# Causal masks written in bf16 by GpSimd, new issue orders for all engines, and a new placing of unused matmuls in a fused linear-attention and MLP kernel

## The chip, the core and the metric

The kernel runs on one core of a Trainium2 chip. The metric is the device time of one execution in microseconds (us); less is better. The engines are named as in the profile: PE is TensorE (matmuls), with PEld for its weight loads; DVE is VectorE, ACT is ScalarE, POOL is GpSimd, and SP is SyncE, which here only issues DMAs. L430 is line 430 of the kernel before.

## The reference

A linear attention with decay feeds a two-layer MLP. Shapes: q, k, v of 4 batches x 8 heads x 768 positions x 64; lam of 8; w_in 512 x 2048, w_out 2048 x 512, alpha 2048; all f32. The output has 3072 tokens x 512.

```python
def _attn_ref(q, k, v, lam):                 # block = 64
    rel = pos[:, None] - pos[None, :]
    Dmask = np.where(rel >= 0, lam[:, None, None] ** rel[None, :, :], 0.0)
    lam_pow = lam[:, None, None] ** (pos[None, :, None] + 1)
    for b in range(nb):
        intra = np.einsum('bhic,bhjc->bhij', qb, kb) * Dmask[None]
        intra = np.einsum('bhij,bhjd->bhid', intra, vb)
        inter = np.einsum('bhid,bhde->bhie', qb * lam_pow[None], kv_state)
        out[:, :, sl] = intra + inter
        kb_dec = kb * rev_pow[None]
        kv_state = lam_block * kv_state + np.einsum('bhsd,bhse->bhde', kb_dec, vb)

def _moe_ref(x, w_in, w_out, alpha):         # x: 3072 x 512, the heads side by side
    h = x @ w_in
    s = np.sin(alpha * h)
    g = h + s * s / (alpha + 1e-09)
    return g @ w_out
```

## The kernel before, in words

**Attention.** The 3072 tokens are 24 blocks of 128 (six of a batch). q is multiplied by powers of lam at load time and k by inverse powers (`scale_block`, L470, L487, L480, L499), so that inside a block the decay needs only a 0/1 mask; v is only cast to bf16 (L493, L502). Each scaled block is transposed on PE (L541 and L518 for q, L568 for k, with `ident` as the second operand) and copied out by ACT or DVE (L546 to L579). Then come S = the products of k and q (`piece_S`, L620), the mask product on DVE (`Sm`, L631), the state Z = v times k (`piece_Z`, L656 and L664) with its bf16 copy into the block-diagonal tile `Zd` (L674), P = Sm times v (L767), I = q times state (L787), and the copy of the sum to `xT` (L734, L747). The first four blocks, the head, are written out piece by piece; the later ones go through the same steps under other lines (L702, L715, L724).

**Decay factors.** Three iotas on POOL make exponents `E_i` (L413 to L417), a cast makes `E_f` (L419), DVE multiplies by ln(lam) (`lnL`, L443), ACT takes four exponentials (`Lq`, `Lp`, `Lk`, L445 to L451) after a table load and a `warm` activation (L442); another table load for the sine follows them (L452).

**Masks.** There are three masks of 128 x 128: two for the head, where positions are interleaved by four, and one for all later blocks. DVE fills one f32 tile `maskf` with ones (L426), POOL's affine_select zeroes what lies above the diagonal (L430, in halves of 64 rows for the first two masks, so five instructions), and DVE casts each to the bf16 `mask` (L435). The identity is made in the same way (L421, L422, L425). POOL also clears the two `Zd` tiles (L438).

**MLP.** Tokens are cut into six chunks of 512. h is computed by units of four 128 x 128 weight tiles against 512 tokens (`unit_A`, L830) or, where half a chunk is ready, of eight matmuls of 256 tokens (`unit_A2`, L864). For each, ACT takes the sine (`t`, L840 or L874), the square is taken by ACT or POOL (`u`, L844, L845, L878, L879) and DVE adds h and multiplies by 1/alpha (`gT`, L847, L882). The first chunk is multiplied by w_out plainly (`unit_B`, L895 and L909); the others by a scheme with fewer matmuls that works on sums of weights (`weight_sums`, L938) and of tokens (`token_sums`, L961) and products of these (`unit_P`, L983, combined in L1000 to L1029).

**Loads.** All DMAs of inputs go through `load` (L325). SP brings q, k, v of the head, the two f32 halves `ws` of the first quarter of w_in (cast by L394 to the first quarter of `w1`), and then q, k, v of later blocks. The other quarters of `w1` and the four of `w2` are brought by POOL's queue, which casts on the way; an issue of such a load takes its turn in POOL's own order, between its squares.

**What sets the order.** Nothing is issued as it is called. `op(...)` records an operation with what it reads and writes, numbered in the order of the calls; a table `ORDER` for each of PE, ACT, DVE, POOL and SP, written out as numbers, then gives the order in which each engine issues them. An operation that more than one engine can do (casts, copies, squares, scalings) goes to the engine in whose table its number stands. `_settle` merges the tables, and `emit` puts a semaphore wait before each operation that depends on another engine's. A pair `(n, cols)` in PE's table stands for n unused matmuls (`spin`, L1142): 128 x 128 by `cols` columns of the tile `idle`, whose result is overwritten later. `idle` is the first part of `Xs_0`, filled by a memset on DVE (L420).

PE's table before begins with 24 unused matmuls, the transposes of k and q with alpha's in between, then by turns the last transposes of k, S of the four blocks and Z of blocks 0, 1 and 2; then P and I of the head with two unused matmuls of 128 columns ahead of the last I, and then the units of the first chunk.

Of the kernel before, what the change touches and what calls it, by code (L numbers as in the profile page):

```python
# [8 lines left out]
F32 = mybir.dt.float32  # L9
# [26 lines left out]
class _Plan:  # L36

    ORDER = {
# [14 lines left out]
        ),  # L53
        "ACT": (
# [15 lines left out]
        ),  # L70
        "DVE": (
# [15 lines left out]
        ),  # L87
        "POOL": (
# [7 lines left out]
        ),  # L96
# [6 lines left out]
        ),  # L103
    }

# [111 lines left out]
def bass_lightning_attn__then__act_snake_kernel(  # L217
# [40 lines left out]
    with es:  # L258

        def sb(name, shape, dt):  # L260
            return es.enter_context(nc.sbuf_tensor(name, shape, dt))
# [27 lines left out]
        Zc = ring("Zc", 2, [128, 4, D], BF16)  # L289
        Zd = ring("Zd", 2, [128, 4, 128], BF16)  # L290
        mask = ring("mask", 3, [128, 128], BF16)
        maskf = sb("maskf", [128, 3, 128], F32)
        ident = sb("ident", [128, 128], BF16)
        identf = sb("identf", [128, 128], F32)
        lam_bc = sb("lam_bc", [128, H], F32)
# [18 lines left out]
        def _(_unused_eng):  # L314
# [4 lines left out]
            op = P.op  # L319
# [103 lines left out]
                out=identf[:, :], in_=identf[:, :], pattern=[[-1, 128]], compare_op=ALU.not_equal,  # L423
                fill=1.0, base=0, channel_multiplier=1), 0.5, ["identf"], ["identf"])
            op("DVE", lambda e: e.tensor_copy(ident[:, :], identf[:, :]), 0.2, ["identf"], ["ident"])  # L425
            op("DVE", lambda e: e.memset(maskf[:, :, :], 1.0), 0.3, writes=[("maskf", i) for i in range(3)])  # L426
            for i in range(3):
                t, ks = (4, 2) if i < 2 else (2, 1)
                for r in ((0, 64), (64, 128)) if i < 2 else ((0, 128),):
                    part = op("POOL", lambda e, i=i, r=r, t=t, ks=ks: e.affine_select(  # L430
                        out=maskf[r[0]:r[1], i, :], in_=maskf[r[0]:r[1], i, :], pattern=[[1, t], [t, 128 // t]],
                        compare_op=ALU.is_ge, fill=0.0, base=-i if i < 2 else 0, channel_multiplier=-ks), 0.3,
                       [("maskf", i)], [("maskf", i)])
                    part.some = i < 2
                op("DVE", lambda e, i=i: e.tensor_copy(mask[i][:, :], maskf[:, i, :]), 0.2, [("maskf", i)], [("mask", i)])  # L435

            for i in range(2):
                op("POOL", lambda e, i=i: e.memset(Zd[i][:, :, :], 0.0), 0.5, writes=[("Zd", i, 0), ("Zd", i, 1)])  # L438
# [818 lines left out]
```

## Time and profile before

| | before |
|---|---|
| median of 3 runs | 212.92 us (212.35 to 214.85) |
| the profiled execution | 213.46 us, of which the span of its records is 211.7 |
| mean granted clock of TensorE | 0.984 |
| DMA | 33.4 MB in 78,999 packets, mean 158 GB/s |
| busiest groups on PE | L830 68.2 us, L983 59.5 us in three groups, L864 23.1 us |
| the chain that ended last | 70% PE, 7% ACT, 7% DVE, 6% DMA, 5% POOL |

A group row of the profile gives line, engine, operation, output and inputs, and count, then busy time and mean ns of one, then the idle time just before and what ended most of it. A row of the timeline gives start and length in us, engine, line, operation and count, and in brackets the wait before it. A row of the chain gives start, length, engine and line. The granted clock is the share of full speed that the chip's throttle gave to TensorE. The rows that matter are shown where they are used.

### The profile page before, as it was taken

How to read it: one execution, taken by the hardware profiler on the slowest of the kernel's cores; microseconds unless marked ns; L12 is line 12 of the kernel's file. 1: busy time of each engine (PE TensorE's matmuls, PEld its weight loads, DVE VectorE, ACT ScalarE, POOL GpSimd, SP SyncE). 2: the span in 40 equal slices, each digit the busy share in tenths (PEclk: the TensorE clock that was granted, in tenths of full speed). 3: DMA queues.
4: the chain of work that ended last, by engine and by line, in shares of the span. 5: the costliest groups of instructions: out<-in, count | busy, mean ns of one | idle time of the engine just before them, and what ended most of it. 6: DMA issues, size and time to landing. Idle time of an engine off the chain costs nothing.

```text
span 211.7 us, 4834 instructions
## 1 busy us (share of the span) xinstructions
PE 202.7 (96%) x1925; PEld 136.4 (64%) x1947; DVE 169.8 (80%) x297; ACT 154.2 (73%) x281; POOL 127.3 (60%) x135
## 2 busy tenths in 40 slices
PE   6979999999999999999999999999999999999994
PEld 2547644555777777667656666765776665677994
DVE  2795496898989999998878987868788666979772
ACT  4685797636999999896988889767975688866000
POOL 6034266713599999698778999398754449022400
PEclk9995899999999999999999999999999999999999
DMA  5999999998899989997999954306400012100424
GB/s 133 305 313 220 186 231 226 231 205 208 177 230 249 291 181 220 224 201 164 200 289 142 242 125 103 97 3 142 156 3 0 3 50 95 54 5 0 174 83 144
DMA packets 78999, 33.36 MB, mean 158 GB/s; under 512 B 55408, under 2 KB 76160, under 8 KB 78976
## 3 DMA queue, kind: packets, MB, share of 16 engines
q1 hardware_dynamic: 74320, 28.19, 57.5%
q0 software_dynamic: 3696, 3.67, 10.7%
q10 hardware_dynamic: 960, 1.19, 2.1%
q8 instruction: 15, 0.25, 0.5%
q14 instruction: 8, 0.07, 0.1%
HBM read 27.28 MB, written 6.29 MB: 159 GB/s over the span
## 4 chain that ended last, share of the span: by engine, by line
PE 70%; ACT 7%; DVE 7%; DMA 6%; POOL 5%; SPq 2%; issue 2%
PE bank L983 24%; PE bank L830 20%; PE bank L864 8%; PE bank L895 6%; POOL gT L961 4%; DMA v<-in_v_dram 3%; ACT t L840 3%; PE bank L724 2%; DMA out_dram<-osb 2%; PE bank L620 2%; SPq L325 2%; DVE gT L882 2%; DVE gT L847 2%; ACT u L844 2%; PE bank L656 1%
## 5 line engine op out<-in xcount | busy, mean ns | idle before, releaser
L830 PE MATMUL bank<-xT,w 128*128 128x512 bf16 x279 | 68.2, 379 | 1.7 <-issue 0.6
L847 DVE SCALAR_TENSOR_TENSOR gT<-u,rinv,bank 128x512 bf16<-128x512 bf16 x74 | 53.9, 743 | 18.1 <-ACT u L844 14.5
L840 ACT ACTIVATE t<-bank,alpha 128x512 bf16<-128x512 f32 x74 | 49.6, 682 | 18.1 <-PE bank L830 16.0
L830 PEld LDWEIGHTS bank<-xT,w 128*128 128x128 bf16 x296 | 27.5, 98 | 28.0 <-DVE gT L847 1.5
L961 POOL TENSOR_TENSOR gT<-gT 128x512 bf16<-128x512 bf16 x31 | 35.7, 1171 | 11.1 <-DVE Xs L961 10.3
L844 ACT ACTIVATE u<-t 128x512 bf16<-128x512 bf16 x61 | 37.9, 629 | 2.1 <-DVE gT L847 0.5
L631 DVE TENSOR_TENSOR Sm<-bank,mask 128x1024 bf16<-128x1024 f32 x24 | 29.0, 1217 | 0.6 <-PE bank L620 0.5
L961 POOL TENSOR_TENSOR Xs<-gT 128x512 bf16<-128x512 bf16 x20 | 23.1, 1168 | 9.2 <-DVE gT L847 9.2
L845 POOL TENSOR_TENSOR u<-t 128x512 bf16<-128x512 bf16 x13 | 13.6, 1047 | 21.1 <-ACT t L840 21.0
L864 PE MATMUL bank<-xT,w 128*128 128x256 bf16 x176 | 23.1, 280 | 0.1
L882 DVE SCALAR_TENSOR_TENSOR gT<-u,rinv,bank 128x256 bf16<-128x256 bf16 x44 | 18.9, 473 | 3.3 <-ACT u L878 2.2
L983 PE MATMUL bank<-w,gT 128*128 128x256 bf16 (+1 forms) x168 | 20.1, 268 | 0.0
L983 PE MATMUL bank<-ws,gT 128*128 128x256 bf16 x160 | 19.9, 273 | 0.0
L874 ACT ACTIVATE t<-bank,alpha 128x256 bf16<-128x256 f32 x44 | 18.3, 476 | 2.1 <-PE bank L864 1.8
L983 PE MATMUL bank<-w,Xs 128*128 128x256 bf16 (+1 forms) x168 | 19.5, 268 | 0.2 <-DVE osb L1029 0.2
L864 PEld LDWEIGHTS bank<-xT,w 128*128 128x128 bf16 x176 | 16.7, 101 | 3.5 <-ACT xT L734 0.3
L983 PEld LDWEIGHTS bank<-w,Xs 128*128 128x128 bf16 x168 | 15.7, 98 | 3.9 <-DVE osb L1029 0.7
L983 PEld LDWEIGHTS bank<-w,gT 128*128 128x128 bf16 x168 | 15.7, 98 | 3.7
L983 PEld LDWEIGHTS bank<-ws,gT 128*128 128x128 bf16 x160 | 15.4, 98 | 3.8 <-DVE osb L1029 0.4
L499 POOL TENSOR_TENSOR qk<-k,Lk 128x512 bf16<-128x512 f32 x16 | 17.4, 1102 | 0.0
L480 POOL TENSOR_TENSOR qk<-q,Lq 128x512 bf16<-128x512 f32 x16 | 17.2, 1082 | 0.0
L895 PE MATMUL bank<-w,gT 128*128 128x512 bf16 x59 | 15.0, 379 | 0.4 <-issue 0.2
(105 smaller groups left out, 270.9 us busy)
## 6 DMA issues: line engine op xcount, KB each, us to landing
k<-in_k_dram SPq DMA_DIRECT2D x24, 256.0 KB, 4.8
q<-in_q_dram SPq DMA_DIRECT2D x12, 512.0 KB, 5.9
v<-in_v_dram SPq DMA_DIRECT2D x24, 256.0 KB, 5.5
out_dram<-osb SPq DMA_DIRECT2D x18, 256.0 KB, 2.4
w<-in_moe_w_out_dram POOLq DMA_DIRECT2D x4, 512.0 KB, 9.7
w<-in_moe_w_in_dram POOLq DMA_DIRECT2D x3, 512.0 KB, 7.1
ws<-in_moe_w_in_dram SPq DMA_DIRECT2D x2, 512.0 KB, 7.1
out_dram<-osb ACTq DMA_DIRECT2D x8, 128.0 KB, 3.9
```

Of the source, the lines that this page charges most:

```text
L499: lambda e: e.tensor_tensor(qk2[:, j, H:2 * H, :], block32(k32, jl), lk, ALU.mult), 1.05,
L631: op("DVE", lambda e: e.tensor_tensor(Sm[js][:, :, :], banks[:, 512 * b0:512 * b0 + 1024].rearrange("p (c i) -> p c i", i=128), bass.AP(ma ...
L830: ins = e.matmul(ps[hb][:, c0:c1], w1[:, kc, 128 * m:128 * (m + 1)], xT[x][:, kc, c0:c1], start=(kc == 0 and c0 == lo), stop=(kc == NKC - ...
L840: op("ACT", lambda e: e.activation(t16[ju][:, w], ps[hb][:, w], ACTF.Sin, scale=alpha[:, m:m + 1]), 0.69 if hi - lo == TCH else 0.475, [ba ...
L844: lambda e: (e.activation(u16[ju][:, w], t16[ju][:, w], ACTF.Square) if e is nc.scalar else e.tensor_tensor(u16[ju][:, w], t16[ju][:, w], ...
L847: op("DVE", lambda e: e.scalar_tensor_tensor(out=gT[g][:, m, w], in0=u16[ju][:, w], scalar=rinv[:, m:m + 1], in1=ps[hb][:, w], op0=ALU.mul ...
L864: ins = e.matmul(ps[hb][:, 256 * i:256 * i + 256], w1[:, kc, 128 * (m + i):128 * (m + i + 1)], xT[x][:, kc, lo:lo + 256], start=(kc == 0 a ...
L874: op("ACT", lambda e, i=i: e.activation(t16[ju][:, 256 * i:256 * i + 256], ps[hb][:, 256 * i:256 * i + 256], ACTF.Sin, scale=alpha[:, m + ...
L882: op("DVE", lambda e, i=i: e.scalar_tensor_tensor(out=gT[g][:, m + i, lo:lo + 256], in0=u16[ju][:, 256 * i:256 * i + 256], scalar=rinv[:, ...
L895: ins = e.matmul(ps[ob][:, w], gT[g][:, m, 128 * s4:128 * (s4 + 1)], w2[:, m, w], start=(m == 0), stop=(m == NM - 1),)
L961: e.tensor_tensor(dst, in0, in1, alu), 0, rd, wr))
L983: ins = e.matmul(ps[ob][:, lo + d0:lo + d1], lhs, rhs[:, d0:d1], start=first and p == 0, stop=(p == NM // 2 - 1), skip_group_check=True)
```

## The change

1. `maskf` is gone. DVE fills each bf16 `mask[i]` with ones, and POOL's five selects write it in place; the three casts L435 are dropped. Operation numbers from there on fall by one.
2. All five tables are new. In the head: SP loads q ahead of k; on POOL all five selects and both clears of `Zd` stand ahead of `E_f`; POOL casts three of the head's four v tiles and ACT one (two and two before), and takes one k scaling from DVE, which takes a state copy; ACT does the cast of `w1`'s first quarter after the last state copies; on DVE the memset of `idle` is first. POOL's weight loads stand so, by quarter: w1[1], w1[2], w2[0], three squares, w1[3], w2[1], one square, w2[2], one square, w2[3]. Before, it was w1[1], w1[2], w2[0], one square, w1[3], three squares, w2[1], w2[2], three squares, w2[3]. The body's units, pieces and evictions are reordered throughout.
3. Unused matmuls: 18 of 512 columns at the start, 3 of 512 ahead of the first S, 1 of 512 ahead of the third S; before, 23 + 1 of 512 at the start and 2 of 128 ahead of the last I.

```diff
         "PE": (
-            (23, 512), (1, 512), 61, 39, 62, 53, 55, 57, 59, 69, 65, 70, 67, 75, 73, 82, 78, 87, 80, 85, 90, 91,
-            (2, 128), 93, 124, 130, 140, 136, 147, 151, 155, 144, 163, 167, 159, 230, 175, 228, 171, 183, 229,
...
+            (18, 512), 54, 58, 38, 56, 52, 60, 61, (3, 512), 64, 68, 69, 66, (1, 512), 72, 74, 77, 81, 79, 84,
+            86, 89, 92, 90, 123, 129, 139, 143, 135, 150, 146, 154, 158, 166, 162, 174, 228, 227, 170, 229, 178,
...
-        maskf = sb("maskf", [128, 3, 128], F32)
...
-            op("DVE", lambda e: e.memset(maskf[:, :, :], 1.0), 0.3, writes=[("maskf", i) for i in range(3)])
             for i in range(3):
+                op("DVE", lambda e, i=i: e.memset(mask[i][:, :], 1.0), 0.2, writes=[("mask", i)])
                 t, ks = (4, 2) if i < 2 else (2, 1)
                 for r in ((0, 64), (64, 128)) if i < 2 else ((0, 128),):
                     part = op("POOL", lambda e, i=i, r=r, t=t, ks=ks: e.affine_select(
-                        out=maskf[r[0]:r[1], i, :], in_=maskf[r[0]:r[1], i, :], pattern=[[1, t], [t, 128 // t]],
+                        out=mask[i][r[0]:r[1], :], in_=mask[i][r[0]:r[1], :], pattern=[[1, t], [t, 128 // t]],
                         compare_op=ALU.is_ge, fill=0.0, base=-i if i < 2 else 0, channel_multiplier=-ks), 0.3,
-                       [("maskf", i)], [("maskf", i)])
+                       [("mask", i)], [("mask", i)])
                     part.some = i < 2
-                op("DVE", lambda e, i=i: e.tensor_copy(mask[i][:, :], maskf[:, i, :]), 0.2, [("maskf", i)], [("mask", i)])
```

107 rows, old and new, of the table ORDER are left out of this document.

## The prediction

> **What bounds the kernel now.** I read the page first, for the share of each engine and the granted clock in 40 slices.
>
> ```profile
> PE 202.7 (96%) x1925; PEld 136.4 (64%) x1947; DVE 169.8 (80%) x297; ACT 154.2 (73%) x281; POOL 127.3 (60%) x135
> PEclk9995899999999999999999999999999999999999
> ```
>
> TensorE is busy for 96% of the span of 211.7 us, so the body is bound by the number of its matmuls, which the change leaves alone. In the slice from 15.9 us the granted clock is 0.5. Next, the table of stretches, cut where the clock changes (steps of 3.41 us fit; it is low from 16.04 to 22.87).
>
> ```profile
> 5.80:9.21 3.41, 3.41 (x20) 1.64 (x18) 2.73 (x6) 2.07 (x6) 0.00 (x0) 1.00 0.97 298
> 9.21:12.63 3.42, 2.77 (x46) 1.83 (x44) 3.33 (x8) 2.76 (x6) 0.00 (x0) 1.00 1.20 303
> 12.63:16.04 3.41, 2.53 (x68) 1.86 (x68) 3.41 (x3) 2.77 (x7) 1.85 (x3) 1.00 1.13 326
> 16.04:19.45 3.41, 3.13 (x75) 2.34 (x68) 1.51 (x3) 1.77 (x4) 2.06 (x4) 0.50 1.16 224
> 19.45:22.87 3.42, 3.42 (x47) 2.76 (x40) 2.91 (x7) 1.19 (x3) 0.00 (x0) 0.50 1.24 205
> 22.87:40.00 17.13, 16.84 (x86) 8.00 (x87) 11.61 (x19) 14.87 (x27) 10.24 (x11) 1.00 1.16 212
> 60.00:205.00 145.00, 143.04 (x1380) 100.66 (x1395) 122.17 (x215) 112.98 (x204) 101.01 (x96) 1.00 0.59 132
> ```
>
> The second column is PE's busy time, the last three are granted clock, DMA share and GB/s. PE was busy for 2.77 and 2.53 of two steps of 3.41; after the second the clock was halved for 6.83 us. From 22.87 on PE idles 0.29 of 17.13 us, and 1.96 of the 145 us after 60: no reordering of the body can win much. DMA is full to 40 and beyond. The chain of waits of the head, and the first matmuls of the MLP (L864):
>
> ```profile
> 5.88 7.08 DMA v<-in_v_dram
> 13.66 0.63 PE bank L656 x8
> 16.59 1.03 PE bank L656 x8
> 17.63 1.00 PE bank L767 x32
> 18.63 0.54 PE bank L787 x4
> 21.35 2.57 PE bank L864 x16
> 52.81 1.75 PE bank L864 x16
> 37.00 2.59 PE bank L830 x12
> ```
>
> The second load of v lands at 12.96, the state matmuls (L656) follow, and from 16.59 the chain is TensorE alone, at half clock: an L656 group takes 1.03 instead of 0.63, and 16 L864 matmuls take 2.57 where the warm ones at 52.81 take 1.75 (0.87 for a unit of 8; an L830 unit of 4 takes 2.59 / 3 = 0.86).
>
> **The masks.** What is removed, what stays, and what the POOL queue also has to make:
>
> ```profile
> L430 POOL TENSOR_SCALAR_AFFINE_SELECT maskf<-maskf 64x128 f32<-64x128 f32 (+1 forms) x5 | 1.5, 307 | 0.3
> L435 DVE CAST mask<-maskf 128x128 bf16<-128x128 f32 x3 | 0.8, 258 | 0.0
> 3.41 0.29 POOL L419 CAST E_f<-E_i 128x128 f32<-128x128 int32 x1
> 4.13 0.52 POOL L438 MEMSET Zd<- 128x512 bf16 x1
> 5.47 0.20 ACT L442 ACTIVATE warm<-lnlam 128x1 f32<-128x1 f32 x1
> 45.17 1.23 DVE L631 TENSOR_TENSOR Sm<-bank,mask 128x1024 bf16<-128x1024 f32 x1 [0.23 <-PE bank L620]
> ```
>
> Three casts of 0.26 leave VectorE. The last stands ahead of the product at 45.17, which then still waits 0.23 for PE; the others lie in the head, where VectorE waits for the exponentials (below) and for q. On the path they are worth nothing. One memset becomes three smaller ones, ahead of that same wait. The five selects stay, in bf16, a form that no row shows: I bound one between 0.15 (half the f32 row, if bytes counted) and 0.6 (twice it), and take the f32 row's 0.31, the same instruction on as many elements. What hangs on it is the queue: E_f now stands behind all five selects and both Zd memsets, two selects and a memset more than before, 2 x 0.31 + 0.52 = 1.14: its cast ends at 3.70 + 1.14 = 4.84. lnL follows (put at 0.26, a mask cast's elements), ready at 5.1; the exponentials cannot run before the warm activation is through at 5.67. So 0.57 are to spare and the delay costs nothing. At 0.6 a select, five add 1.45: the exponentials 0.9 late, of which I let 0.4 reach the MLP.
>
> **The unused matmuls.** 24 + 2 become 18 + 3 + 1.
>
> ```profile
> 1.93 7.25 PE L1142 MATMUL bank<-Xs 128*128 128x512 bf16 x24 [1.93 <-DVE Xs L420]
> ```
>
> The 24 end at 9.18, 0.30 each. Eighteen end about 1.8 earlier, at 7.4, less the 0.4 by which the memset of their operand comes earlier: 7.0. PE then waits for the first scaled tile, at most the 2.2 until 9.18. The three and the one stand where PE waits for ScalarE's copies, and cost nothing; the two that go stood on the path, 0.2 warm (0.22 each, an L830 matmul).
>
> **The head's order.** SP loads q before k; both land as early together as before, since DMA is full. The first L656 still waits for the second v, now cast by POOL instead of ScalarE: 13.7 again. The next bound is VectorE's four mask products:
>
> ```profile
> 12.59 3.49 DVE L631 TENSOR_TENSOR Sm<-bank,mask 128x1024 bf16<-128x1024 f32 x3
> 16.35 1.23 DVE L631 TENSOR_TENSOR Sm<-bank,mask 128x1024 bf16<-128x1024 f32 x1 [0.27 <-PE bank L620]
> 14.31 0.76 ACT L674 CAST Zd<-bank 64x256 bf16<-64x256 f32 x2 [0.22 <-PE bank L656]
> 16.56 1.04 ACT L394 CAST w<-ws 128x1024 bf16<-128x1024 f32 x1
> ```
>
> VectorE loses a k scaling of 512 columns (to POOL) and gains a state copy of 256; by the products' 1.16 per 1024 columns that is 0.3 net. So the first product starts near 12.2; four in a row and the copy (0.3 to 0.4) end at 12.2 + 4.64 + 0.35 = 17.2, where the old four ended at 17.58. Then one L767 group (1.00 at half clock, 0.5 warm) and two L787 groups (0.27 each warm) end at 18.2. The w1 cast on ScalarE, now behind two more state copies (0.76), ends at 17.60 + 0.76 = 18.4. The MLP starts at 18.4 instead of 21.35, and its first two units take 1.75 instead of 2.57: done at 20.15, not 23.92. That is **3.77 us**, if the clock stays at 1.00. If it halves from 16.04 to 22.87 again, the start is 18.4 + 0.8 for the groups at half clock, 19.2, the two units take twice 1.75 and end at 22.7: 1.2 us.
>
> **Whether the clock stays.** The step that brought the fall was 2.53 busy and the one before it 2.77. The new order puts three unused matmuls (0.65) into the first, which is then full, and one into the second: 2.75, about what the first had before, plus the products and state groups that now come earlier. I take it that the clock stays, at 2 to 1. PE's longest single wait in there was half a us:
>
> ```profile
> PE bank L656 <- ACT Zd L674: 0.8, 2, 0.5
> ```
>
> [...]
>
> **What is late next: the weights.** The body's first part needs w1 and w2 quarter by quarter, which POOL's queue loads between its squares.
>
> ```profile
> 26.37 0.80 POOL L325 DMA_DIRECT2D w<-in_moe_w_in_dram  x1
> 30.94 1.55 POOL L325 DMA_DIRECT2D w<-in_moe_w_out_dram  x2
> L845 POOL TENSOR_TENSOR u<-t 128x512 bf16<-128x512 bf16 x13 | 13.6, 1047 | 21.1 <-ACT t L840 21.0
> w<-in_moe_w_in_dram POOLq DMA_DIRECT2D x1, 512.0 KB, 7.1
> w<-in_moe_w_out_dram POOLq DMA_DIRECT2D x1, 512.0 KB, 7.3
> w<-in_moe_w_out_dram POOLq DMA_DIRECT2D x1, 512.0 KB, 10.6
> w<-in_moe_w_out_dram POOLq DMA_DIRECT2D x1, 512.0 KB, 8.8
> 39.59 0.86 PE bank L895 x4
> 42.90 0.81 PE bank L895 x3
> 48.24 0.81 PE bank L895 x3
> ```
>
> The four loads, with their KB and us to landing, are in order those issued at 26.37 (w1's last quarter, lands 33.5), 30.94 (w2's second, 38.2), about 31.7 (w2's third, 42.3) and 37.3, after three more squares (w2's last, 46.1). The old order first uses w2's second at 39.59, its third at 42.90 and its last a unit after 48.24, at 49.1: slack 1.4, 0.6 and 3.0. So the new order, 3.77 earlier, runs into the loads. Before w2's second quarter it has one L830 unit less (0.86): PE is there at 20.15 + 39.59 - 23.92 - 0.86 = 34.96 and, with landings as before, waits until 38.2, 0.5 ahead of the old kernel. It also wants w2's last quarter earlier: two units (1.72) and a step of attention (1.1, by an L656 group of 0.63 and two L787 groups of 0.27) come after it now. Landing still at 46.1, it lets PE go on at 46.2 with 2.8 still owed: 49.0, level with the old 49.1. **The gain is then what the loads come earlier, x.**
>
> POOL's queue: w1's last and w2's second quarter now follow three squares, one directly after the other. In the old kernel w1's last was issued 26.37 - 21.35 = 5.0 behind the MLP's start, after one square; 0.8 of this was half clock. With two more squares of 1.05 (the L845 row) the new issues come at 18.4 + 4.2 + 2.1 = 24.7 and 25.5, 1.7 and 5.4 earlier. If the loads still wait for all that SP brings, x is 0; if nothing but their issue counted, the 3.77 arrive whole. I take x from the first of the two, **1.7**: the landings lay 4.7, 4.1 and 3.8 apart, so it is the engines that space them (DMA share 1.16), and a queue that starts 1.7 sooner with the same spacing stays 1.7 ahead. 38.2 becomes 36.5, and 34.96 is still below it: the loads, not the head, decide.
>
> SP's queue moves along: q of the next blocks still waits for w1's third quarter, then k, v, v in the old order. Their scalings on VectorE and POOL stand ahead of evictions, so a late k or v would hold those up; I cost it at zero, as DMA brings the same bytes by the same time, and keep it for the slow end. The body's other reorderings have 0.29 + 1.96 of idle to win, or as much to lose; I take zero.
>
> **Sum.** The profiled execution took 213.46 (211.7 of span and 1.76 around it), 0.54 over the median of 212.92. 213.46 - 1.7 = 211.76, or against the median **211.2**. A measurement of this kernel tells about 2% from no change, 4.3 us; this is 0.8%.
>
> **The rivals.**
> 1. The loads land as before (x = 0) and the head's gain is spent waiting for w2: 213.46 + 0.4 of new small waits, 213.3 beside the median. For it: the full DMA engines; against: the earlier issues. 0.2.
> 2. The loads come as early as their issue and the head's 3.77 arrives whole: 209.2. For it: the first gap, 4.7, was wider than the last, 3.8, so there was room. 0.15.
> 3. The clock falls all the same at 16.04: the head gains 1.2, which the loads allow: 211.7. 0.15.
> 4. The slow side: the clock closes a step earlier. Behind the eighteen PE waits up to 2.2 for scaled tiles; if that makes the step from 5.80 count as low, half clock runs from 9.21 to 22.87. Two L656 groups (0.4 more each) and what lies before the MLP slip about as much again: the MLP starts 1.7 later than the old 21.35, at 23.0, its two units are warm and end at 24.8, 0.9 behind the old kernel, and the late E_f's 0.4 comes on top: 214.2. It decides where the step from 5.80 has PE busy for less than the 2.53 that brought the fall, a hole over 0.9. 0.1.
>
> [...]
>
> That the change does not do what it says is possible only as case 3. My forecast holds the remaining 0.4.
>
> **Numbers.** Range: from a body that wins 0.5 beyond case 2 to case 4 with the selects at 0.6 (0.4 more): 208.7 to 214.7, which takes in x from 0 to 3.77. Faster by over 2% is under 208.7: the far end of case 2, 0.13. Slower by over 2% is over 217.2: only if k or v starve for some 5 us behind the bunched weights, 0.07. Within: 0.80.
>
> **What would show it.** Granted clock 1.00 from 12.6 to 23; L656's first group at 13.7; the first MLP group at 18.4; E_f's cast ending before 5.4 and selects near 0.31; w1's last and w2's second quarter issued near 24.7 and 25.5 and landing near 31.8 and 36.5; PE waiting about 1.5 us at the first use of w2's second quarter and little elsewhere. I would be wrong if PE waits for k or v between 40 and 50, if the clock halves before 12.6, or if PE's idle time after 60 differs by more than 1 us from 1.96.

## The result

| | median, us | runs | ratio to before (95% interval) |
|---|---|---|---|
| before | 213.25 | 20 | |
| changed | 215.45 | 20 | 1.0109 (1.008 to 1.0138) |

The change makes the kernel 1.1% slower, 2.3 us. The forecast was 0.8% faster, with a range that ended at 214.7. The profiled execution took 215.03, of which 213.3 is its span. Ratios, here and below, leave out runs that are more than 1.5% above the fastest of the same kernel, while medians take all runs. The table of stretches of the changed kernel (length, busy time of PE, PEld, DVE, ACT, POOL, then granted clock, DMA share, GB/s):

```profile
9.21:12.63 3.42, 3.30 (x62) 2.28 (x61) 3.27 (x7) 2.05 (x5) 1.98 (x3) 1.00 1.20 290
12.63:16.04 3.41, 3.16 (x86) 2.18 (x87) 3.41 (x5) 2.56 (x7) 2.24 (x4) 1.00 1.12 332
16.04:19.45 3.41, 2.13 (x50) 1.46 (x50) 2.86 (x6) 2.76 (x5) 1.13 (x2) 1.00 1.25 229
19.45:22.87 3.42, 2.88 (x14) 2.06 (x14) 0.32 (x2) 0.84 (x2) 0.26 (x1) 0.51 1.24 204
22.87:40.00 17.13, 17.13 (x87) 7.83 (x86) 9.73 (x16) 13.40 (x23) 12.15 (x12) 1.00 1.17 209
40.00:60.00 20.00, 18.40 (x186) 11.19 (x184) 18.84 (x29) 13.33 (x28) 8.24 (x7) 1.00 1.10 234
60.00:205.00 145.00, 143.90 (x1381) 100.19 (x1379) 119.91 (x204) 112.04 (x203) 111.86 (x107) 1.00 0.55 127
```

Three differences from the table of before. The clock is low in one step, 19.45 to 22.87, instead of two. From 22.87 to 40 PE is never idle: it waits for no weights. From 40 to 60 it is busy 18.40 us where it was 19.73, by this row of before:

```profile
40.00:60.00 20.00, 19.73 (x196) 12.46 (x197) 18.30 (x31) 12.83 (x25) 8.69 (x8) 1.00 0.96 213
```

The chain of waits of the changed kernel shows both places, the start of the MLP and the wait behind it:

```profile
18.55 0.28 PE bank L863
18.83 1.17 issue
20.00 3.23 PE bank L863 x15
...
51.93 0.69 DVE qkT L550
52.62 2.57 DVE qk L498
55.24 0.40 PE bank L517 x4
```

The MLP starts at 18.55 (forecast 18.4), stops after one matmul for 1.17 us with nothing to wait for that the profile shows, and then runs at half clock: its first two units end at 23.23 and not at 20.15; the old kernel had them at 23.92. At 51.9 the chain leaves PE for VectorE, which scales k for 2.57 us.

The mean granted clock of the 20 runs is 1.00 in eight (median 214.4) and 0.991 or 0.992 in twelve (215.6): the fall of the clock comes and goes from run to run, and the two groups lie 1.2 us apart. The fall does not explain the loss, since it costs the kernel before more. That kernel ran 104 times beside the experiments below, on four chips. Its clock was 1.00 in 21 of these runs, with medians of 211.0 to 211.8 us by chip; 0.99 in 40, with 212.2 to 213.2; 0.98 in 42, with 213.4 to 214.3; and 0.97 in one. At full clock the changed kernel is so 2.6 to 3.4 us behind. A ratio below can also come from how often a kernel kept the clock, and where it changes the reading, the runs of equal clock are compared.

### The profile page after: what moved, and what is told of

It is laid out like the page before. It is cut to its first block, busy times and chain, and to the rows that moved or that the text cites. A ratio compares the mean times of both kernels' runs of the same rounds, so it can differ in the third digit from the quotient of the medians.

```text
span 213.3 us, 4848 instructions
## 1 busy us (share of the span) xinstructions
PE 203.5 (95%) x1943; PEld 135.0 (63%) x1943; DVE 165.9 (78%) x284; ACT 152.4 (71%) x280; POOL 141.7 (66%) x148
## 3 DMA queue, kind: packets, MB, share of 16 engines
q1 hardware_dynamic: 74320, 28.19, 56.6%
q10 hardware_dynamic: 960, 1.19, 1.9%
## 4 chain that ended last, share of the span: by engine, by line
PE 85%; DVE 6%; ACT 5%; issue 2%; POOL 1%; ACTq 0%; POOLq 0%
PE bank L829 30%; PE bank L982 28%; PE bank L863 8%; PE bank L894 7%; PE bank L619 3%; PE bank L723 3%; ACT t L873 1%; PE bank L701 1%; DVE qk L498 1%; PE bank L540 1%; DVE Sm L630 1%; DVE qk L469 1%; PE bank L517 1%; PE bank L655 1%; ACT u L877 1%
## 5 line engine op out<-in xcount | busy, mean ns | idle before, releaser
L829 PE MATMUL bank<-xT,w 128*128 128x512 bf16 x296 | 71.9, 380 | 0.7 <-DVE xT L733 0.7
L839 ACT ACTIVATE t<-bank,alpha 128x512 bf16<-128x512 f32 x74 | 50.2, 683 | 21.6 <-PE bank L829 20.8
L960 POOL TENSOR_TENSOR gT<-gT 128x512 bf16<-128x512 bf16 x34 | 39.1, 1162 | 14.3 <-DVE Xs L960 11.9
L843 ACT ACTIVATE u<-t 128x512 bf16<-128x512 bf16 x60 | 37.2, 628 | 1.9 <-DVE gT L846 0.2
L960 POOL TENSOR_TENSOR Xs<-gT 128x512 bf16<-128x512 bf16 x22 | 25.5, 1170 | 2.5 <-DVE gT L846 2.5
L863 PE MATMUL bank<-xT,w 128*128 128x256 bf16 x176 | 23.8, 285 | 1.6 <-issue 1.2
L844 POOL TENSOR_TENSOR u<-t 128x512 bf16<-128x512 bf16 x14 | 14.7, 1054 | 14.5 <-ACT t L839 12.1
L479 POOL TENSOR_TENSOR qk<-q,Lq 128x512 bf16<-128x512 f32 x16 | 17.4, 1094 | 0.0
L894 PE MATMUL bank<-w,gT 128*128 128x512 bf16 x64 | 15.6, 379 | 0.0
```

What stands on the lines that cost most here:

```text
L829: ins = e.matmul(ps[hb][:, c0:c1], w1[:, kc, 128 * m:128 * (m + 1)], xT[x][:, kc, c0:c1], start=(kc == 0 and c0 == lo), stop=(kc == NKC - ...
L839: op("ACT", lambda e: e.activation(t16[ju][:, w], ps[hb][:, w], ACTF.Sin, scale=alpha[:, m:m + 1]), 0.69 if hi - lo == TCH else 0.475, [ba ...
L843: lambda e: (e.activation(u16[ju][:, w], t16[ju][:, w], ACTF.Square) if e is nc.scalar else e.tensor_tensor(u16[ju][:, w], t16[ju][:, w], ...
L863: ins = e.matmul(ps[hb][:, 256 * i:256 * i + 256], w1[:, kc, 128 * (m + i):128 * (m + i + 1)], xT[x][:, kc, lo:lo + 256], start=(kc == 0 a ...
L894: ins = e.matmul(ps[ob][:, w], gT[g][:, m, 128 * s4:128 * (s4 + 1)], w2[:, m, w], start=(m == 0), stop=(m == NM - 1),)
L960: e.tensor_tensor(dst, in0, in1, alu), 0, rd, wr))
```

## Experiments

Three parts to test, masks, head and body, and inside these the stop at 18.83 and the scaling at 52.6.

**Masks alone.** The kernel before in its own orders, with the three memsets where the one was and the casts left out:

```diff
-            op("DVE", lambda e: e.memset(maskf[:, :, :], 1.0), ...)
+                op("DVE", lambda e, i=i: e.memset(mask[i][:, :], 1.0), ...)
-                op("DVE", lambda e, i=i: e.tensor_copy(mask[i][:, :], maskf[:, i, :]), ...)
```

> The kernel before with only the masks changed: three bf16 memsets in place of the one of f32, selects on bf16, no casts; all orders as before. Masks are worth nothing: ratio 0.998 to 1.002, selects near 0.31 us. Rival: a bf16 select in place is dearer and delays the exponentials: selects over 0.45 and ratio over 1.002.

213.32 us, ratio 1.0018 (0.9981 to 1.0055): no difference, as expected. The view of the line of the selects (min/median/max in ns), in bf16:

```profile
L429 POOL TENSOR_SCALAR_AFFINE_SELECT mask<-mask x5: 303/308/316, 1.6 to 18.0; 64x128 bf16<-64x128 bf16 x4, 128x128 bf16<-128x128 bf16 x1
```

**Head and body apart.** Two mixtures of the tables: each engine's table is cut at its first MLP operation; one kernel has the changed part ahead of the cut and the old behind it, the other the reverse. For PE (the bar shows the cut and is no code):

```diff
-        "PE": ((18, 512), 54, 58, ... 92, 90, | 123, 129, 139, 143, 135, ...)
+        "PE": ((18, 512), 54, 58, ... 92, 90, | 123, 129, 139, 135, 146, ...)
```

> Every engine issues the head (all that is called before the first MLP unit) in the changed kernel's order, with its masks and its unused matmuls, and the rest in the order of the kernel before. Theory A (two separate losses: a head whose gain shrank from 3.8 to 0.7 us, and a body that is 2.5 us slower): the MLP's first two units end near 23.2 as in the changed kernel, nothing is lost behind them, and the time is 0.5 to 1.5 below the kernel before, ratio 0.993 to 0.998. Rival B (the head alone is to blame, by its clock and its gap): about the changed kernel's time, ratio 1.008 to 1.014.

> The head in the order of the kernel before (its unused matmuls too, masks in bf16), the rest in the changed kernel's order. Theory A: the body costs 2.5 us, 1.9 of it in PE's wait for k scalings near 52 us; ratio 1.009 to 1.014. Rival B: the body is even, ratio 0.997 to 1.003.

The old head with the new body: 215.46, ratio 1.014 (1.0089 to 1.019). The body alone costs the loss, as theory A had it. A part of this ratio is the clock: five of its six runs had 0.98 and a median of 215.5, the kernel before on the same chip 213.7 in its twelve runs of that clock, 1.8 us less. The new head with the old body missed both forecasts upwards: 215.55, ratio 1.0155 (1.0096 to 1.0214). Its chain says why:

```profile
48.91 5.31 DMA v<-in_v_dram
```

SP's part ahead of the cut also holds loads of k and v for the blocks behind the head; in the changed order the v that the old body needs near 50 us is the last of them. So this run tells about an order of loads that fits no body. (The old head with the new body has the reverse, old loads for a new body, but in its profile PE waits for no load; its longest wait, 1.6, is for VectorE.) Once more with SP's table cut behind the head's own loads:

> As the first mixture (changed head, body of before), but SP's loads for the blocks behind the head stand in the order of the kernel before; in the first mixture they stood in the changed order, and PE waited 5.3 us for a v that SP issued at 48.9. Theory A: that wait is gone, PE waits less than 1 us between 40 and 60, and the head's gain shows: ratio 0.990 to 0.999. Rival D (whatever the order, q, k and v for the blocks from 50 us on cannot land sooner, because the DMA engines are full to 57, so a head that is 1 to 2 us ahead waits for them): PE still loses 1 to 2 us between 46 and 58; ratio 0.999 to 1.004.

212.03, ratio 0.9956 (0.9909 to 1.0004). The new head is worth about 0.4%, 0.9 us, though its interval just reaches 1; at full clock it is 211.4 (seven runs) against 211.8 (eight runs of the kernel before on that chip), half a us. The rest of the way to 1.0109, 1.5%, is the body's, and the old head with the new body (1.4%) agrees; by the runs of equal clock it is 1.8 to some 3 us. The expectations further down call this kernel, the new head with the old body and its loads, the second mixture; here it is the head mixture.

**The scaling at 52.6.** The timeline of the changed kernel on VectorE, GpSimd and PE:

```profile
52.54 3.24 DVE L498 TENSOR_TENSOR qk<-k,Lk 128x512 bf16<-128x512 f32 x2
52.52 2.11 POOL L937 TENSOR_TENSOR w<-w 128x1024 bf16<-128x1024 bf16 x1
55.24 0.40 PE L517 MATMUL bank<-ident,qk 128*128 128x128 bf16 x4 [1.60 <-DVE qk L498]
```

Two k scalings take 3.24 us, of which the first takes 2.64. In the kernel before one takes 0.68 on VectorE (the group's row: busy us, mean ns of one, idle time before it):

```profile
L499 DVE TENSOR_TENSOR qk<-k,Lk 128x512 bf16<-128x512 f32 x4 | 2.7, 682 | 0.0
```

The two begin together with a weight sum on GpSimd that takes 2.11, and the first ends half a us after it. In the kernel before that sum (L938) ran on VectorE. One number moved:

```diff
         "DVE": (
-            ... 210, 331, 250, 212, 218, ...
+            ... 210, 331, 332, 250, 212, 218, ...
         "POOL": (
-            ... 261, 332, 284, ...
+            ... 261, 284, ...
```

> The changed kernel with one weight sum (the one GpSimd runs at 52.5 for 2.1 us) done by VectorE in its 0.85 us hole at 51.1 instead. Theory A (the k scaling on VectorE that starts at 52.54 took 2.64 instead of 0.68 because GpSimd's sum held something both use): the scaling takes 0.68, PE goes on near 53.4 instead of 55.2, and the time falls by 1.5 to 1.9 us against the changed kernel; ratio to the kernel before 1.001 to 1.005. Rival C (the scaling waited for something else, or the time is given back at a later wait): less than 0.5 us, ratio 1.008 to 1.013.

213.81, ratio 1.0041 (1.0002 to 1.0081): 0.7% or 1.4 us back, theory A, a little less than it said. The scalings did not fall to 0.68 each, since they now meet a scaling on GpSimd:

```profile
50.96 2.33 DVE L498 TENSOR_TENSOR qk<-k,Lk 128x512 bf16<-128x512 f32 x2
51.26 1.49 POOL L498 TENSOR_TENSOR qk<-k,Lk 128x512 bf16<-128x512 f32 x1
```

The old head with the new body, which keeps the sum on GpSimd, has the slow scalings at another time, so it is not the head that brings them:

```profile
53.53 3.36 DVE L497 TENSOR_TENSOR qk<-k,Lk 128x512 bf16<-128x512 f32 x2
53.77 2.57 POOL L936 TENSOR_TENSOR w<-w 128x1024 bf16<-128x1024 bf16 x1
```

The traces show a delay in both directions, but not what makes it. In the 17 profiles of this case 34 scalings of q or k on VectorE took more than 0.75 us, and every one of them ended 0.546 to 0.554 us after the end of a GpSimd operation beside it; the other 224 took less. In the rows above, the first scaling begins at 53.53 and, at the 0.68 of an undelayed one, runs to 54.21 at least; GpSimd's sum is taken up at 53.77, while it runs, and takes 2.57 instead of 2.11, as if it began when the scaling was nearly over. The second scaling then ends at 56.89, 0.55 after the sum.

In the changed kernel's profile the same pattern stands at 139, beside a token sum, ahead of a copy of xT that PE waits for:

```profile
138.97 1.44 DVE L960 TENSOR_TENSOR Xs<-gT 128x512 bf16<-128x512 bf16 x1
138.97 1.15 POOL L960 TENSOR_TENSOR Xs<-gT 128x512 bf16<-128x512 bf16 x1
141.11 2.79 PE L829 MATMUL bank<-xT,w 128*128 128x512 bf16 x12 [0.66 <-DVE xT L733]
```

With the copy put ahead of that token sum on VectorE, besides the first repair:

```diff
         "DVE": (
-            ... 739, 767, 770, 752, 751, ...
+            ... 739, 767, 752, 770, 751, ...
```

> The changed kernel with the weight sum on VectorE, as before, and with the copy of xT that PE waits for at 141.1 put ahead of the token sum that took 1.44 us on VectorE beside GpSimd's. Theory A: PE's wait of 0.66 at 140.5 is gone; 0.5 to 1.0 below the run with the weight sum alone; ratio 0.997 to 1.002. Rival C: given back later, ratio 1.002 to 1.006.

213.07, ratio 0.9994 (0.996 to 1.0028), 0.5% below the run with the first repair alone. That this is the second repair's is not shown. The two intervals overlap. In the profile with the first repair alone the wait is gone already, because there the token sum on VectorE was first, by 0.01, and took 0.42:

```profile
136.94 0.42 DVE L960 TENSOR_TENSOR Xs<-gT 128x512 bf16<-128x512 bf16 x1
136.96 1.43 POOL L960 TENSOR_TENSOR Xs<-gT 128x512 bf16<-128x512 bf16 x1
```

And the run with both kept the clock in ten runs of twelve, the other in five of twelve; at full clock they are 1.0 (212.86 against 211.84) and 1.4 us (212.39 against 211.00) behind the kernel before on their own chips. So of the body's 3.2 us (1.5%) the first repair gives back 1.4, and the rest, 1.8 or less, was not located. The profiles with one and with both repairs show one wait more that the changed kernel has not, 0.76 and 0.68 near 107 for an addition on VectorE (L1028; 0.24 in the kernel before), and no run tests it.

**The stop at 18.83.** One packet of 16 KB on an instruction queue falls in there (the DMA view of the changed kernel, 17 to 22 us: count, MB, share of 16 engines; 1.6% is 1.3 us of one engine):

```profile
q8 instruction: 1, 0.02, 1.6%
```

Counting matmuls, weight loads and semaphore instructions, PE stops at its 448th or 449th (in the changed kernel's trace 220 matmuls, 221 weight loads and 8 others lie ahead of the stop). The number of unused matmuls ahead shifts that place; one kernel has 24 at the start, another 8 in the same way:

```diff
-            (18, 512), 54, 58, 38, ...
+            (24, 512), 54, 58, 38, ...
```

> The changed kernel with 24 unused matmuls at the start instead of 18. Theory F (PE's gap of 0.9 to 1.2 us inside the first MLP unit, after its first matmul, is the end of the code that PE has loaded: a 16 KB instruction packet that starts at 17.36 and takes 1.30): 12 more instructions lie ahead, so the gap comes 12 instructions earlier, inside the two L786 groups at 17.5 to 18.1, and ends at 19.5 to 20 again. Rival G (the gap belongs to the MLP's first unit, its bank or its weights): it stays behind the first L863 matmul. Time within 0.5 of the changed kernel.

> The changed kernel with 8 unused matmuls at the start instead of 18. Theory F: 20 instructions fewer, so the gap comes behind the 11th L863 matmul and shrinks to 0.3 or less or is gone; the first MLP units end 0.5 to 1.1 earlier unless the clock falls for want of the unused matmuls. Rival G: the gap stays behind the first L863 matmul at 0.9 to 1.2.

PE's timeline with 24, and with 8:

```profile
17.75 0.40 PE L786 MATMUL bank<-qkT,Zd 128*128 128x128 bf16 x4
19.90 0.61 PE L786 MATMUL bank<-qkT,Zd 128*128 128x128 bf16 x4 [1.76 <-issue]
```

```profile
19.50 1.92 PE L863 MATMUL bank<-xT,w 128*128 128x256 bf16 x16 [0.45 <-ACT w L394]
```

With 24 the stop moves ahead into the L786 groups, as theory F says, and is longer, 1.76; with 8 it is gone. Wherever PE stops, it goes on at 19.7 to 20.1. The times: 215.81 with 24 (1.012, 1.0071 to 1.0169), 213.69 with 8 (1.0006, 0.9956 to 1.0055). Not all of the latter is the stop's: there the sum on GpSimd began at 52.9, after the scaling at 51.3, and PE lost little at that place (19.46 busy from 40 to 60). The first two units end at 21.42; in the profile with the weight sum moved, which has the stop but kept the clock, they end at 21.53. So what the stop costs by itself is small, as the head with 8 comes to the MLP 0.95 later.

**The four unused matmuls in the middle.**

```diff
-            (18, 512), 54, 58, 38, 56, 52, 60, 61, (3, 512), 64, 68, 69, 66, (1, 512), 72, ...
+            (18, 512), 54, 58, 38, 56, 52, 60, 61, 64, 68, 69, 66, 72, ...
```

> The changed kernel without its four unused matmuls ahead of S (18 at the start stay). If they hold the clock: PE is busy for about 2.6 of the step from 9.21 to 12.63 and the clock is halved from 12.63 or 16.04 on, as in the kernel before; 1 to 2 us over the changed kernel, ratio 1.015 to 1.022. If they do not: the clock is as in the changed kernel, the gap moves 8 instructions on (behind the 5th L863 matmul), and the time is within 0.5; ratio 1.008 to 1.013.

213.14, ratio 1.0045 (1.0017 to 1.0074), and the timeline:

```profile
18.56 0.72 PE L863 MATMUL bank<-xT,w 128*128 128x256 bf16 x5 [0.45 <-ACT w L394]
20.09 1.36 PE L863 MATMUL bank<-xT,w 128*128 128x256 bf16 x11 [0.81 <-issue]
```

The stop comes after the fifth matmul, as forecast, and is 0.81. The clock was 1.00 throughout, in all ten runs: the four do not hold it. It fell in none of the 22 runs of this kernel and of the fastest one below, against twelve of 20 of the changed kernel and five of 12 of the head mixture, which differ from them by the four: with them PE stops after the first matmul of the MLP and not after the fifth, in both for 1.17 instead of 0.8. The time was forecast unchanged (1.008 to 1.013) and is 0.6% less. How much of that is due to the four was not separated, as here too GpSimd's sum began behind the scalings, at 52.8 (19.52 busy from 40 to 60).

**What the head is worth without the stop.** On the old body with its loads:

> The second mixture (changed head, body and body loads of before) with 8 unused matmuls at the start instead of 18. Theory F: PE's gap at its 448th instruction goes as it did in the changed kernel with 8, the first MLP units end 0.5 to 1.5 earlier, and the old body turns part of it into time: ratio 0.988 to 0.996. Rival D: what the head gains is spent waiting for loads between 40 and 58, ratio 0.995 to 1.000.

211.65, ratio 0.9948 (0.9921 to 0.9975). With 8 at the start the clock fell early (0.53 from 9.21 to 12.63), and the MLP started at 19.81 but did not stop. The gain over the kernel before lies in what a fall costs, not in a shorter path: its five runs with a fall have 210.8 to 212.0, while its seven at full clock have a median of 211.6 against 211.0 of the kernel before on that chip (six runs).

> The changed kernel with both body repairs and 8 unused matmuls at the start. If the gains add up (0.5 to 1.0 us of the 18 to 8, 2.3 of the two repairs): ratio 0.990 to 0.998. If the body takes the head's gain back: 0.998 to 1.001.

213.01, ratio 1.0022 (0.9992 to 1.0052): the gains do not add up on the changed body; in its profile the MLP started at 20.44, 1.9 later than with 18.

```diff
-        idle = Xs[0][:, 0, 0:2, :].rearrange("p a b -> p (a b)")
+        idle = sb("idle32", [128, 256], F32)[:, :]
-            (18, 512), 54, 58, 38, 56, 52, 60, 61, (3, 512), 64, 68, 69, 66, (1, 512), 72, ...
+            (9, 256), 54, 58, 38, 56, 52, 60, 61, (3, 128), 64, 68, 69, 66, (1, 128), 72, ...
```

> The second mixture with the unused matmuls in f32: 9 of 256 columns at the start and 3 + 1 of 128, on a tile of their own, which should last as long with 18 instructions fewer. If an f32 matmul takes about four times a bf16 one of its width: the clock is as with 18, the gap comes 18 instructions later and is 0.3 or less, first MLP matmul at 18.5, units done at 20.5 to 21; ratio 0.986 to 0.996. If the f32 ones last longer than that, the first transposes start late and the head loses 1 us or more.

212.69, ratio 1.0004 (0.9971 to 1.0036), a miss. An f32 matmul counts as two in the records (6 for 3), so no instructions were saved, and the stop was 2.17. The nine at the start took 6.79 us and the three 0.89, where the 18 of 512 columns in bf16 took 6.19 in the changed kernel and its three 0.81.

Last, the head mixture with 18 at the start and no unused matmuls in the middle:

> Changed head without its four unused matmuls ahead of S (18 at the start stay), body of before. Theory F: the gap stands behind the 5th matmul of the MLP's first unit and is 0.8; the clock stays at 1.00 where it fell in the run with them; first two units done at 21.5. If the changed kernel's gain of 0.6% from leaving the four out holds here too: ratio 0.988 to 0.994. If not: 0.994 to 0.998.

211.09, ratio 0.993 (0.99 to 0.9961): the fastest of all, and faster than both kernels. Its stretches, and in its chain the row that answers to the 37.00 of before:

```profile
16.04:19.45 3.41, 2.56 (x54) 1.84 (x54) 2.86 (x6) 2.76 (x5) 1.07 (x2) 1.00 1.25 229
19.45:22.87 3.42, 2.81 (x19) 1.85 (x19) 0.71 (x3) 2.25 (x6) 0.00 (x0) 1.00 1.24 204
40.00:60.00 20.00, 20.00 (x219) 12.91 (x217) 18.23 (x30) 14.30 (x29) 9.04 (x10) 1.00 1.09 234
```

```profile
34.52 2.59 PE bank L828 x12
```

The clock stays, two units of the MLP end at 21.43 (20.06 + 1.37), 2.5 ahead of the old kernel, and 2.5 ahead the old body stays: 34.52 against 37.00, with PE never idle from 40 to 60. No load is late. That is against a profile of before with the clock halved for 6.83 us. All twelve runs of this kernel kept the clock; the four of 17 in which the kernel before kept it on that chip have a median of 211.7, 0.6 above 211.09. So more than half of the gain is the clock that stays.

> As the one before, with 12 unused matmuls at the start: 12 instructions fewer, so the gap comes behind the 11th matmul and is 0.2 or less. If PE's early clock stays at 1.00: first two units done at 20.6 to 21.0, ratio 0.986 to 0.993. If it falls between 5.8 and 12.6, as with 8: the MLP starts 1 us later, ratio 0.992 to 0.997.

No ratio: its six runs lie between 209.84, the only one at full clock, and 216.44; the others have 0.96 or 0.97. In its profile the clock was 0.50 to 0.59 from 9.21 to 22.87, behind a step in which PE was busy for 1.64 of 3.41 us, and the MLP started at 21.75.

**What the packet waits for.**

```diff
         "POOL": (
-            ... 47, 51, 101, 102, 104, 126, 141, ...
+            ... 47, 51, 126, 101, 102, 104, 141, ...
```

> The changed kernel with GpSimd's first three weight loads (issued at 14.7 to 16.4) behind its first square, some 23 us. One look, for the instruction packet alone; the time will be 2 us or more longer, as the weights come late. Theory F1 (the packet, due when PE passes its 231st instruction at 14.2, waits until 17.3 because the DMA engines are full of those loads and of SP's): with three loads fewer it starts earlier than 16.5 and the gap shrinks under 0.6 or is gone. Rival F2 (what it waits for are SP's loads, which were issued before): it starts at 17.0 to 17.4 as in every run so far, gap 0.8 to 1.2.

218.21 in a single run. In its DMA view from 17 to 22 us (40 slices) the engines run empty at 17.4, and the stop is what it was:

```profile
DMA  9991000000000000000000000000000004000000
```

```profile
20.00 3.11 PE L863 MATMUL bank<-xT,w 128*128 128x256 bf16 x15 [1.17 <-issue]
```

So GpSimd's loads are not what the packet waits for, as rival F2 had it. In every trace with the new head it began at 17.1 to 17.4, and in the three with the old head at 16.8 to 17.3. That it waits behind SP's loads, which had just ended in this run, fits but was not shown by itself.

## Why the prediction was wrong

**Masks: right.** Selects 0.31, nothing on the path. The delay of E_f was mis-sized: its cast ended at 5.68, not 4.84, and the first exponential began at 6.04, where the warm activation had left 5.67. Little of it can have reached the MLP, whose first matmul came at 18.55, not 18.4.

```profile
5.39 0.29 POOL L419 CAST E_f<-E_i 128x128 f32<-128x128 int32 x1
6.04 0.23 ACT L444 ACTIVATE Lq<-lnL 128x32 f32<-128x32 f32 x1 [0.36 <-DVE lnL L442]
```

**"The MLP starts at 18.4 ... done at 20.15": the start was right, the end failed.** PE's code was not in the sum. The old kernel comes to its 448th only at 20.6, when the packet is long through (16.96 + 1.08 = 18.04); a head that is 2.8 us faster is there at 18.83, just behind the packet's end (17.36 + 1.30 = 18.66), and goes on at 20.00. With the stop, PE was busy for 2.13 of the step from 16.04, and the clock fell in the next; in the profiles of the two repaired kernels it was busy for 2.14 and 2.13 and the clock stayed, so the share alone does not decide it.

**"Whether the clock stays" failed as a step.** It was argued from the steps of one profile and from busy times of 2.53 against 2.75. No run shows a busy time of a step at which the clock falls: in two profiles with 8 unused matmuls at the start PE was busy for 0.74 and 0.95 of the step from 5.80, and the next had 0.53 in one (head mixture) and 1.00 in the other (both repairs). The fall came in 12 of 20 runs; the unused matmuls that were to prevent it do not (2.65 and 2.83 busy without them, clock 1.00).

**"The loads, not the head, decide" was wrong.** PE waited for no weights in the changed kernel. Their issues hang on POOL's squares and these on the MLP's start, so they follow the head: w1's last and w2's second quarter were issued at 27.38 and 28.19, not 24.7 and 25.5, since the head itself was late,

```profile
27.38 0.81 POOL L325 DMA_DIRECT2D w<-in_moe_w_in_dram  x1
28.19 0.75 POOL L325 DMA_DIRECT2D w<-in_moe_w_out_dram  x1
```

and in the fastest mixture, 2.5 ahead, they came in time. (With the new body and a head that lost less, as with 8 at the start, PE waited 0.3 to 0.4 for a quarter of w2.) Rival 2 had this right, x close to the head's gain.

**"The body's other reorderings ... I take zero" is the step that decided the sign.** It cost 1.4 to 1.5%, 3.2 us by the ratios and at least 1.8 at equal clock; one place where VectorE stood beside a weight sum on GpSimd makes 1.4 of it, and the cause of the rest stays open. The bound that I read from PE's idle time (2.25 us, to win or as much to lose) was none for a loss, and it was too large for a gain: the page of before has 1925 matmuls to 1947 weight loads, the changed one 1943 to 1943, so a part of that idle time is matmuls that the records lack. That GpSimd does a weight sum and more token sums in the new order could be read in the tables, and the slow side of the rivals should have been this and not the clock.

## What to carry to other kernels

When an order moves work to GpSimd, look in the new order for what VectorE does at the same time and who waits for that: here the cost sat in VectorE's own durations (2.64 us for a scaling that took 0.68), not in a wait of its own, and the group's mean of 1.19 hid it. Compare runs of equal granted clock before you give a difference to an edit. A denser head can stop at a place where the old one did not, as here for 1.17 us at the 449th instruction: count the instructions up to the first stop that has no releaser, and see whether an instruction packet ends beside it (here at 18.66, 1.3 before PE went on). Test a schedule in parts that belong together: a body goes with the order of its loads.

## What the runs showed of the hardware

PE's code seems to come in packets of 16 KB. The changed kernel's trace has 15 of them on one queue; from the second, which begins near PE's 487th instruction by the same count, to the last near the 3752nd they lie 251 apart on average (174 to 321), which is why I take them for PE's. By this estimate the first was due some 250 ahead of the 487th, at 14.2 (256 ahead, the gap to the third, gives the 231st of theory F1); it began at 17.4 and took 1.3. In the ten traces with a stop PE went on 1.3 to 1.6 after the packet's end, and where the packet began at 17.06 instead of 17.36, PE went on at 19.73 instead of 20.00. The stops were 0.8 to 2.2 us long. What delays the packet stays open.

The clock's steps lie differently from run to run: the kernel with the masks alone shows 0.80 and 0.70 in two neighbouring steps of the grid of before, where 0.50 stood in both.

```profile
16.04:19.45 3.41, 2.98 (x88) 2.20 (x89) 2.64 (x4) 2.42 (x6) 2.27 (x4) 0.80 1.17 222
19.45:22.87 3.42, 3.42 (x46) 2.95 (x38) 2.69 (x6) 1.55 (x4) 0.00 (x0) 0.70 1.24 206
```

One profile cannot tell whether the clock will hold: it fell in twelve of the changed kernel's 20 runs.
